# First batch of an attention and SwiGLU kernel: grouped softmax, moved weight rounding, Newton root

## Chip, cores and metric

The kernel runs on one core of a Trainium2 chip. The metric is the device time of one launch in microseconds (us); the profile's span is the profiled execution alone.

## The reference, cut to what matters

Attention with 32 learnt queries over 12,416 rows, then the rows attend to the 32 results, then a gated feed-forward layer on every row:

```python
B, N, m, C = 4, 12416, 32, 128          # x: (B, N, C); inducing: (m, C)
def mab(q, kv):
    s = scale * (q @ kv.transpose(0, 2, 1))
    s = s - s.max(-1, keepdims=True)
    a = np.exp(s)
    a /= a.sum(-1, keepdims=True) + 1e-09
    return a @ kv
h = mab(I, x)                            # I: inducing, once per batch
y = mab(x, h).reshape(B * N, C)
rms = np.sqrt(np.mean(y * y, axis=-1, keepdims=True) + 1e-06)
xn = y / rms * rms_g
g = xn @ w_gate                          # C -> 1536
out = (g / (1 + np.exp(-g))) * (xn @ w_val) @ w_out
```

`w_gate`, `w_val` and `w_out` come as 64-bit floats, the other inputs as 32-bit floats.

## The kernel before, in words

The 97 tiles of 128 rows of a batch form seven sets: five of 16 tiles (0 to 4), one of 15 (5) and one of 2 (6, the set that the code calls `full`). In the second attention and in the feed-forward layer a set is worked in units of up to 512 columns; a unit has 12 slots, one per 128 of the 1536 hidden channels. A slot does `g` (L677), silu on ACT (L685), `v` (L688), their product on DVE (L694), and adds products with `wo` (L613) to the unit's accumulator, either at once ("plain") or split in three faster products ("three", L629 to L670).

Every engine gets its instructions in the order in which the Python code issues them. For batches 1 to 3 all of the attention's steps are laid between the slots by `schedule` and the steps of a list of slot numbers; for batch 0 there is nothing yet to lay them between, so the main part (L703 to L803) writes out the order by hand. That part is the start, and it is what the change touches:

1. x comes in by SP's queue, set after set (`load_rows`), and set 6 in four pieces at the end. Between and behind them come the raw weights in chunks of 128x512 64-bit words (`fetch_raw`); five chunks have a place at once, the other four are fetched as places become free.
2. `turn_x` transposes a set's tiles on TensorE, four to a PSUM bank, and ACT copies each bank to SBUF (L316). There are five such banks. `scores1` multiplies with the 32 queries and DVE takes the scores out together with each row's maximum (L326).
3. `max1`, `max2`, `max3` bring the maximum over all sets to every partition: a reduction on DVE, a transpose on TensorE, two short operations on DVE, a product on TensorE, a copy. The bias of the exponential needs it, and so the exponentials (`exp1_of`, L355) begin after the last set's scores.
4. `turn_e` transposes the exponentials on DVE, `sum_h` adds their products with x in one bank (L378), `fold_l` adds the denominators, `divide` divides (L393), `turn_h` and `square_h` prepare the second attention.
5. The seam of set 0: scores, maximum, exponential, `turn_a`, `square`, `turn_z`, `scale`, `root` (on POOL, a power of -0.5, L516), `apply`, `turn_b`, `split`. Set 0's first unit gets its input `a` by `spread` (two products, one ACT copy, L558); the next two units get theirs by `gather`, four SBUF to SBUF transfers each on SP (L545).
6. Then the slots begin; slots 0 to 3 belong to unit 0, 4 to 7 to unit 1, 8 to 11 to unit 0 again, and so on for the first two units; set 0's later units begin at slot 24.

Rounding the weights to 32 bits (`rounding`) is a side job. A chunk's high word is cut by DVE into exponent (L249) and upper fraction (L262); ACT makes numbers of them (L229, L231; for two chunks DVE does so, L233); DVE puts the sign on (L271) and adds the low word (L277); POOL multiplies (L279) and `put` stores the chunk (L221, for `w_gate` and `w_val`) and fetches the next raw one. There are nine chunks, three of each weight, named (weight, chunk) in the order (0,0), (1,0), (2,0), (0,1), ... Five are rounded before the slots or in the first of them, four in slots 1 to 14. `stack_of` multiplies a rounded chunk with h to make the first layer's matrices for batch 0, `stack_low` takes a part of the rounding error off. `warm` issues idle matmuls.

A planner (`rehearse`) goes through all slots with a table of costs (`COST`) and decides which products take the three-product form and where in a slot products are issued. For batch 0 it allows the form from the third unit and slot 26 on.

## Time and profile before

| | |
|---|---|
| median of 3 runs | 1623.13 us (1622.79 to 1623.69) |
| span of the profiled execution | 1621.7 us |
| PE busy | 1604.3 us, 99% |
| DVE, ACT, POOL busy | 1444.6, 1238.3, 1217.7 us |
| first silu of the first slot | 56.02 us |
| last sum of h ends | 38.46 us |

PE is TensorE; PEld its weight loads, which overlap; DVE VectorE, ACT ScalarE, POOL GpSimd, SP the sync engine, whose queue issues most transfers. Busy time of a matmul is modelled from pipelined records, so a busy TensorE is one that has work queued. The mean of a line can mix shapes. The start takes 55 of 1622 us, and shares over the whole span hide it: it is read alone, by timelines and by stretches.

### The profile page before, as it was taken

How to read it: one execution, taken by the hardware profiler on the slowest of the kernel's cores; microseconds unless marked ns; L12 is line 12 of the kernel's file. 1: busy time of each engine (PE TensorE's matmuls, PEld its weight loads, DVE VectorE, ACT ScalarE, POOL GpSimd, SP SyncE). 2: the span in 40 equal slices, each digit the busy share in tenths (PEclk: the TensorE clock that was granted, in tenths of full speed). 3: DMA queues.
4: the chain of work that ended last, by engine and by line, in shares of the span. 5: the costliest groups of instructions: out<-in, count | busy, mean ns of one | idle time of the engine just before them, and what ended most of it. 6: DMA issues, size and time to landing. Idle time of an engine off the chain costs nothing.

```text
span 1621.7 us, 25435 instructions
## 1 busy us (share of the span) xinstructions
PE 1604.3 (99%) x7085; PEld 1085.6 (67%) x7085; DVE 1444.6 (89%) x2504; ACT 1238.3 (76%) x2285; POOL 1217.7 (75%) x979
## 2 busy tenths in 40 slices
PE   8999999999999999999999999999999999999998
PEld 6546666756676666766677666676667777777776
DVE  4879988999899998899899998789989999999997
ACT  4567877767887778776778777877778888878886
POOL 1358885878588886688678888587858878878876
PEclk9999999999999999999999999999999999999999
DMA  7455624444353141634445323353221122111221
GB/s 262 91 72 85 112 43 97 88 97 69 60 94 59 36 95 29 133 76 81 69 67 83 55 54 68 63 125 79 46 38 29 31 39 40 35 35 36 40 38 26
DMA packets 389181, 112.52 MB, mean 69 GB/s; under 512 B 365072, under 2 KB 369712, under 8 KB 386480
## 3 DMA queue, kind: packets, MB, share of 16 engines
q1 hardware_dynamic: 388304, 110.82, 34.8%
q8 instruction: 56, 0.92, 0.3%
q14 instruction: 85, 0.70, 0.2%
q10 hardware_dynamic: 736, 0.08, 0.0%
HBM read 53.95 MB, written 27.00 MB: 50 GB/s over the span
## 4 chain that ended last, share of the span: by engine, by line
PE 94%; DVE 1%; ACT 1%; issue 1%; POOL 0%; DVEq 0%; ACTq 0%
PE acc L613 35%; PE gv L677 18%; PE gv L688 16%; PE u L635 10%; PE u L633 10%; PE gv L322 3%; PE gv L499 1%; PE gv L378 1%; DVE gv L694 1%; ACT silu L685 1%; PE gv L453 0%; DVE xn L660 0%; PE gv L467 0%; DVE o L621 0%; POOL xn L279 0%
## 5 line engine op out<-in xcount | busy, mean ns | idle before, releaser
L669 POOL TENSOR_TENSOR xn<-xn,xn 128x512 fp32r<-128x512 f32 (+2 forms) x705 | 870.9, 1255 | 268.6 <-DVE xn L660 156.8
L685 ACT ACTIVATE silu<-gv 128x512 f32<-128x512 f32 (+2 forms) x1186 | 689.7, 586 | 258.4 <-PE gv L677 231.8
L688 PE MATMUL gv<-a,sv 128*128 128x512 f32 (+2 forms) x1188 | 636.1, 536 | 0.8 <-ACT silu L685 0.8
L613 PE MATMUL acc<-u,wo 128*128 128x512 f32 (+1 forms) x990 | 490.8, 581 | 0.0
L677 PE MATMUL gv<-a,sg 128*128 128x512 f32 (+2 forms) x1188 | 486.7, 410 | 1.5 <-ACT silu L685 0.8
L694 DVE TENSOR_TENSOR u<-silu,gv 128x512 f32<-128x512 f32 (+2 forms) x621 | 407.7, 663 | 51.7 <-PE gv L688 32.3
L694 DVE TENSOR_TENSOR gv<-silu,gv 128x512 f32<-128x512 f32 (+2 forms) x565 | 376.0, 668 | 66.1 <-PE gv L688 49.0
L660 DVE SCALAR_TENSOR_TENSOR xn<-xn,gv 128x512 fp32r<-128x512 f32 (+2 forms) x566 | 371.3, 656 | 9.5 <-ACT xn L659 5.9
L659 ACT ACTIVATE xn<-gv 128x512 fp32r<-128x512 f32 (+2 forms) x566 | 330.4, 584 | 43.1 <-DVE gv L694 30.9
L677 PEld LDWEIGHTS gv<-a,sg 128*128 128x128 f32 x1188 | 223.8, 188 | 189.4 <-ACT silu L685 40.2
L688 PEld LDWEIGHTS gv<-a,sv 128*128 128x128 f32 x1188 | 223.6, 188 | 139.6 <-issue 46.3
L613 PE MATMUL acc<-xn,more 128*128 128x512 f32 (+2 forms) x705 | 273.6, 388 | 3.0 <-DVE o L621 2.6
L633 PE MATMUL u<-xn,xn 128*128 128x512 f32 (+2 forms) x705 | 272.4, 386 | 0.0
L613 PEld LDWEIGHTS acc<-u,wo 128*128 128x128 f32 x990 | 184.9, 188 | 46.7 <-issue 9.1
L664 POOL TENSOR_TENSOR xn<-u,xn 128x512 fp32r<-128x512 f32 (+2 forms) x139 | 178.6, 1285 | 41.6 <-ACT xn L663 41.6
L635 PE MATMUL u<-xn,xn 128*128 128x512 f32 (+2 forms) x414 | 160.1, 387 | 0.0
L613 PEld LDWEIGHTS acc<-xn,more 128*128 128x128 f32 x705 | 132.4, 188 | 33.5 <-POOL xn L669 5.7
L633 PEld LDWEIGHTS u<-xn,xn 128*128 128x128 f32 x705 | 132.6, 188 | 28.6 <-issue 5.5
L663 ACT ACTIVATE xn<-u 128x512 fp32r<-128x512 f32 (+2 forms) x139 | 87.4, 629 | 36.6 <-DVE u L694 32.4
L635 PE MATMUL u<-xn,more 128*128 128x512 f32 (+2 forms) x291 | 112.5, 387 | 0.0
L516 POOL TENSOR_TENSOR rs<-ms,mhalf 128x16 f32<-128x16 f32 (+2 forms) x28 | 75.9, 2709 | 18.1 <-DVE ms L511 17.1
L635 PEld LDWEIGHTS u<-xn,xn 128*128 128x128 f32 x414 | 77.7, 188 | 17.5 <-DVE gv L694 0.2
(151 smaller groups left out, 1096.9 us busy)
## 6 DMA issues: line engine op xcount, KB each, us to landing
out_dram<-o SPq DMA_DIRECT2D x320, 64.0 KB, 2.0
xT<-in_x_dram SPq DMA_DIRECT2D x60, 256.0 KB, 5.4
xn<-in_x_dram SPq DMA_DIRECT2D x60, 256.0 KB, 5.0
a<-hi SPq DMA_DIRECT2D x156, 64.0 KB, 2.0
a<-lo SPq DMA_DIRECT2D x156, 64.0 KB, 2.0
xn<-in_x_dram SPq DMA_DIRECT2D x5, 1024.0 KB, 10.6
xn<-w SPq DMA_DIRECT2D x18, 256.0 KB, 3.6
out_dram<-o SPq DMA_DIRECT2D x64, 60.0 KB, 2.0
```

What stands on the lines that cost most here:

```text
L613: nc.tensor.matmul(acc[:, 0:T], lhsT, rhs, start=st["left"] == NJ, stop=st["left"] == 1)
L633: nc.tensor.matmul(ups[:, 0:T], weight_of(0, j), hi, start=st["k"] == nk, stop=False)
L635: nc.tensor.matmul(ups[:, 0:T], weight_of(1, j), lo, start=False, stop=not st["k"])
L659: nc.scalar.activation(hi, v, AF.Copy, scale=(1.0 - 2.0 ** -13) * 2.0 ** -12)
L660: nc.vector.scalar_tensor_tensor(out=lo, in0=hi.bitcast(F32), scalar=-4096.0, in1=v, op0=ALU.mult, op1=ALU.add)
L663: nc.scalar.activation(d, v, AF.Copy, scale=1.0 - 2.0 ** -13)
L664: nc.gpsimd.tensor_tensor(out=lo, in0=v, in1=d.bitcast(F32), op=ALU.subtract)
L669: nc.gpsimd.tensor_tensor(out=d, in0=hi.bitcast(F32), in1=lo.bitcast(F32), op=ALU.subtract)
L677: nc.tensor.matmul(g[:, 0:T], sg[:, ts(j, P)], a[:, 0:T], start=True, stop=True)
L685: nc.scalar.activation(sl[:, 0:T], g[:, 0:T], AF.Silu)
L688: nc.tensor.matmul(v[:, 0:T], sv[:, ts(j, P)], a[:, 0:T], start=True, stop=True)
L694: nc.vector.tensor_tensor(out=t[:, 0:T], in0=sl[:, 0:T], in1=v[:, 0:T], op=ALU.mult)
```

## The change

In words:

- Batch 0's first softmax is taken in three groups of sets (0 to 2, 3 and 4, 5 and 6), each with its own maximum, exponential and PSUM bank; `shares` computes exp(bias difference) for each group, and `divide` joins the three sums with these factors. The order of the start is written anew, with sums of early groups between the transposes of later sets.
- Set 6 is loaded first, from ACT's queue, and transposed after set 0. Set 5 is loaded in two parts. All raw weights are fetched after x.
- Every second bank of transposes is copied by DVE instead of ACT.
- Rounding a chunk is now two masks on DVE, four operations on ACT (power, upper part, sign, low word) and three on POOL (`join`); only (1,0) keeps the old joining with two DVE operations (`join_short`). Before the slots, (0,1) and (1,1) are rounded later than they were; within them the chunks are at slots 0 to 12 instead of 0 to 14.
- The root of the first seam is computed by an integer first guess and three Newton steps on DVE, 12 short operations.
- The planner's table follows; `wo` is split from slot 15 (17), and the three-product form is allowed from slot 25 (26).

The diff, cut:

```diff
+    GROUPS = (range(0, 3), range(3, 5), range(5, NS))
...
-                nc.sync.dma_start(out=t[ts(q, m), 0:n, :], in_=of(xrows, b, s)[q])
+                (nc.sync if b else nc.scalar).dma_start(out=t[ts(q, m), 0:n, :], in_=of(xrows, b, s)[q])
...
+        def join():
+            if wide:
+                e, f = st["e"].bitcast(F32), st["f"].bitcast(F32)
+                nc.gpsimd.tensor_tensor(out=f[:], in0=f[:], in1=st["low"].bitcast(F32), op=ALU.add)
+                nc.gpsimd.tensor_tensor(out=e[:], in0=e[:], in1=st["high"].bitcast(F32), op=ALU.mult)
+                nc.gpsimd.tensor_tensor(out=st["dst"], in0=f[:], in1=e[:], op=ALU.mult)
+            put()
...
-                nc.scalar.copy(out=dst, in_=src)
+                if k % 2:
+                    nc.vector.tensor_copy(out=dst, in_=src)
+                else:
+                    nc.scalar.copy(out=dst, in_=src)
...
+        def shares():
+            G = len(st["parts"])
+            least = small.tile([P, 1], F32, name="mx")
+            nc.vector.tensor_reduce(out=least[:], in_=st["nb"][:], axis=AX.X, op=ALU.min)
+            share = st["share"] = small.tile([P, G], F32, name="rl")
+            nc.scalar.activation(share[:], st["nb"][:], AF.Exp, bias=least[:], scale=-1.0)
+            ls = st["ls"][:, 0:G]
+            nc.vector.tensor_tensor(out=ls, in0=ls, in1=share[:], op=ALU.mult)
+            nc.vector.reduce_sum(out=st["hl"][:, C:C + 1], in_=ls, axis=AX.X)
...
+    def first_root(ms, rs):
+        n = small.tile([P, 16], I32, name="mx2")
+        y, t = rs, small.tile([P, 16], F32, name="mx2")
+        nc.vector.tensor_scalar(out=n[:], in0=ms.bitcast(I32), scalar1=1, scalar2=None, op0=ALU.logical_shift_right)
+        nc.vector.tensor_scalar(out=y.bitcast(I32), in0=n[:], scalar1=-1.0, scalar2=float(0x5F3759DF),
+                                op0=ALU.mult, op1=ALU.add)
+        nc.vector.tensor_scalar_mul(out=ms, in0=ms, scalar1=-0.5)
+        for _ in range(3):
+            nc.vector.tensor_tensor(out=t[:], in0=y, in1=y, op=ALU.mult)
+            nc.vector.tensor_tensor(out=t[:], in0=t[:], in1=ms, op=ALU.mult)
+            nc.vector.scalar_tensor_tensor(out=y, in0=t[:], scalar=1.5, in1=y, op0=ALU.add, op1=ALU.mult)
...
+    turn_x(0, *range(R))
+    f["scores1"](0)
+    turn_x(NS - 1, 0)
+    turn_x(1, *range(R))
+    f["scores1"](NS - 1)
+    turn_x(2, *range(R))
+    f["scores1"](1)
+    f["scores1"](2)
+    f["max1"](0)
+    turn_x(3, *range(R))
+    f["max2"]()
+    f["max3"](0)
+    f["exp1_of"](0, 3, 0)
+    f["scores1"](3)
+    f["turn_e"](0)
+    turn_x(4, *range(R))
+    f["sum_h"](0)
+    f["scores1"](4)
+    f["max1"](1)
+    turn_x(5, 0, 1)
+    f["max2"]()
+    turn_x(5, 2, 3)
+    f["max3"](1)
+    f["exp1_of"](3, 5, 1)
+    f["turn_e"](1)
+    f["scores1"](5)
+    f["max1"](2)
+    f["sum_h"](1)
+    f["turn_e"](2)
+    f["max2"]()
+    weight[0, 0]["masks"]()
+    f["sum_h"](2)
+    f["max3"](2)
+    numbers(0, 0)
+    f["exp1_of"](5, NS, 2)
+    f["turn_e"](3)
+    f["sum_h"](3)
+    f["turn_e"](4)
+    f["sum_h"](4)
+    weight[0, 0]["join"]()
+    f["turn_e"](5)
+    f["turn_e"](6)
+    f["shares"]()
+    weight[1, 0]["masks"]()
+    f["fold_l"]()
+    f["sum_h"](5)
+    f["sum_h"](6)
+    numbers(1, 0, False)
+    for g in range(len(GROUPS)):
+        f["divide"](g)
     f["turn_h"]()
     ps = f["scores"](0, f["st"]["hT"][:, 0:m], R, per2[0])
     f["square_h"]()
-    weight[2, 0]["sign"]()
-    f["stack_of"](0, 0)
+    weight[1, 0]["join_short"]()
     warm(10)
     f["scores2"](0, ps)
+    f["stack_of"](0, 0)
     f["row_max"](0)
     f["sub_max"](0)
-    weight[2, 0]["lower"]()
+    weight[2, 0]["masks"]()
     f["exp2"](0, 1)
     tiny = small.tile([P, 1], F32, name="tiny")
     nc.scalar.activation(tiny[:], ones, AF.Silu)
+    numbers(2, 0)
+    weight[2, 0]["join"]()
     turn_a, square, turn_z, scale, root, apply, turn_b, split = seam(0, 0)
     turn_a()
     square()
-    parts(0, 1)
+    weight[0, 1]["masks"]()
     f["stack_of"](1, 0)
-    warm(26)
+    warm(20)
     turn_z()
     scale()
     root()
-    weight[0, 1]["sign"]()
-    for i in range(2):
-        f["stack_low"](i, 0)
-    parts(1, 1)
     apply()
     turn_b()
     split()
     spread(0, 0)
+    numbers(0, 1)
+    weight[0, 1]["join"]()
+    for i in range(2):
+        f["stack_low"](i, 0)
     warm(3)
     gather(0, 1)
     gather(0, 2)
-    weight[0, 1]["lower"]()
+    weight[1, 1]["masks"]()
+    numbers(1, 1)
+    weight[1, 1]["join"]()
...
-            for k, one in ((1, (2, 1)), (5, (0, 2)), (8, (1, 2)), (11, (2, 2))):
-                for j, name in ((0, "power"), (1, "power_number"), (1, "upper"), (2, "upper_number"), (2, "sign"), (3, "lower")):
-                    add(k + j, weight[one][name])
-            for k, *one in ((2, 0, 1), (4, 1, 1), (11, 0, 2), (13, 1, 2)):
+            for k, one in ((0, (2, 1)), (3, (0, 2)), (6, (1, 2)), (9, (2, 2))):
+                for j, name in enumerate(("masks", "power_number", "upper_number", "sign_number", "lower_number", "join")):
+                    add(k + (j + 1) // 2, weight[one][name])
+            for k, *one in ((2, 0, 1), (4, 1, 1), (9, 0, 2), (12, 1, 2)):
```

## The prediction

> **What bounds the kernel now.** I read the page first: its chain of waits says what ends last.
>
> ```profile
> span 1621.7 us, 25435 instructions
> ...
> PE 94%; DVE 1%; ACT 1%; issue 1%; POOL 0%; DVEq 0%; ACTq 0%
> ```
>
> TensorE is the bound, and nothing in the change takes matmuls out of the long middle. So the question is when TensorE gets into its stride. Busy time by stretches shows the stages of the start (columns: stretch, its length, PE, PEld, DVE, ACT and POOL busy with counts, clock, DMA share, GB/s):
>
> ```profile
> 8.17:25.64 17.47, 16.02 (x140) 11.35 (x138) 5.25 (x15) 12.08 (x25) 0.00 (x0) 1.00 1.00 395
> 25.64:31.53 5.89, 5.41 (x50) 4.32 (x50) 5.50 (x17) 1.91 (x4) 1.27 (x1) 1.00 0.40 109
> 31.53:38.46 6.93, 6.70 (x197) 5.43 (x196) 5.44 (x13) 3.37 (x8) 1.29 (x1) 1.00 0.29 83
> 38.46:54.25 15.79, 13.30 (x92) 10.19 (x91) 13.54 (x25) 6.52 (x13) 4.56 (x2) 1.00 0.19 64
> 54.25:62.40 8.15, 7.65 (x26) 4.40 (x27) 6.29 (x11) 4.86 (x9) 2.76 (x3) 1.00 0.55 148
> ...
> 110.00:1600.00 1490.00, 1485.71 (x6315) 1008.67 (x6314) 1354.57 (x2325) 1167.82 (x2152) 1178.95 (x934) 1.00 0.34 64
> ```
>
> Transposes and scores; the maximum's chain (most of that TensorE time is warm-up matmuls); the sums of h; the seam, a chain through DVE; the first slots. Past 110 us TensorE idles 4.3 us in 1490. A microsecond won or lost before about 62 us therefore stays won or lost at the end.
>
> Then the timelines of DVE, POOL, ACT and SP, one by one, around the change's places (start, length, engine, line, operation):
>
> ```profile
> 48.12 0.68 DVE L271 SCALAR_TENSOR_TENSOR we<-sg,we 128x512 int32<-128x512 int32 x1
> ...
> 59.99 0.92 DVE L262 TENSOR_SCALAR o<-sc 128x512 int32<-128x512 int32 x1
> ```
>
> ```profile
> 48.29 3.29 POOL L516 TENSOR_TENSOR rs<-ms,mhalf 128x16 f32<-128x16 f32 x1 [3.25 <-DVE ms L511]
> ...
> 54.98 1.28 POOL L279 TENSOR_TENSOR xn<-o,we 128x512 f32<-128x512 f32 x1 [3.40 <-PE gv L555]
> ...
> 59.28 1.34 POOL L279 TENSOR_TENSOR xn<-o,we 128x512 f32<-128x512 f32 x1 [2.88 <-PE gv L677]
> ```
>
> ```profile
> 54.84 0.58 ACT L558 CAST a<-gv 128x512 fp32r<-128x512 f32 x1 [2.98 <-PE gv L555]
> ...
> 56.02 1.58 ACT L685 ACTIVATE silu<-gv 128x512 f32<-128x512 f32 x3 [0.59 <-PE gv L677]
> ```
>
> ```profile
> 58.00 0.59 SPq L545 DMA_DIRECT2D xn<-lo  x1
> 58.69 0.53 SPq L221 DMA_DIRECT2D w<-xn  x1
> 59.31 0.40 SPq L209 DMA_DIRECT2D sg<-in_moe_w_out_dram  x1
> ```
>
> Three things to see. ACT has nothing between the copy of `a` and the first silu. The store of the weight that POOL finished at 56.26 goes out at 58.69, behind the eight gathers written ahead of it: SP keeps the program's order. And L262, whose median is 0.42, takes 0.92 while a POOL operation runs to 60.62, and ends 0.29 after it.
>
> **What the skill says.** SBUF — State Buffer, "Who interferes with whom": DVE and GpSimd share a port pair, a lock for a whole instruction; one-source DVE operations in a 2-port mode and those with two SBUF inputs contend. The trace agrees for the first kind (0.92 above; L249 has 0.90 and 0.80 beside POOL); for the second it hints: the power after L271 took 3.29, the median of its line is 2.90. PSUM — Partial Sum Buffer, "Engine vs sequencer instructions": ScalarE, VectorE and GpSimd queues are strict FIFO; every timeline here follows program order. DMA: Bandwidth & Descriptors, "Queues, rings and completion order": each DMA engine takes turns between queues. The trace agrees: `gam`, 0.5 KB on ACT's queue behind `ind`, needed 8.8 us, and between 4.5 and 10.0 us its queue moved 144 packets beside x.
>
> **The change, part by part.** Before and after are walked down the program's order with durations of this trace, an instruction starting when its engine is free and its inputs are there. For the kernel before this gives the division at 39.3; it ended at 38.87. I subtract the 0.4 below.
>
> *Three groups, copies on two engines.* TensorE's work up to the last sum: 97 transposes at 0.115 (11.2), scores 97/16 x 0.97 (5.9), sums 97 x 0.065 (6.3), small products about 0.9: 24.3. From 8.17 that ends at 32.5 without waits. The order has these waits, 6.0 together: 0.9 for the copies of set 0; 1.2 before the first `max3` (DVE still has set 2's scores and two copies of set 3, 0.6 to 0.75 each, ahead of the two row operations); 0.5 before set 5's scores; 0.5 before set 2's sum; 1.2 before set 3's sum, since `exp1_of` of group two waits for group two's bias while DVE is busy; 0.9 before `fold_l`, since group three's exponential stands behind four rounding operations of 0.5 to 0.63 on ACT, and `shares` is four short dependent steps; the rest small. A DVE copy of 128x512 from PSUM is not in the trace: taken as 0.66 from L326, the same form with a maximum; 0.55 to 0.75 moves the sum by under 1 us. With the last two divisions (0.75) the division ends at 39.3 - 0.4 = 38.9. So the hidden chain (4.8 us, 26.7 to 31.5) is paid back in DVE's longer queue: 0, between -4 (half of the waits overlap more than I think, the exponential is not delayed) and +1.
>
> *Set 6 on ACT's queue, asked for right after set 0.* Before it landed at 22.7 and nobody waited. Now its 128 rows follow `gam` (10.0) in ACT's queue, in turn with x's packets of 8 KB (0.31 each): eight rounds per engine, 2.5 to 5 us, so about 13.5. TensorE reaches `turn_x` of set 6 at 11.85: +1.7. If a piece has to wait on ACT for an older transfer to land (SP did so at 6.07 and 10.0), ACT's table load and copies slip too: the walk then gives +2.0. Bounds 0 and +5. Fetching the weights behind x gains nothing here: x's sets 1 to 5 are transposed at TensorE's pace already.
>
> *Port lock in `shares`.* POOL's three products of weight (0,0), 1.25 each, run just then. The product `ls x share` and the two masks behind it meet two of them: +1.5 (0 to 1.7).
>
> *Seam.* Joining (1,0) puts two 0.6 operations on DVE ahead of the transpose of the scores, masks (2,0) two of 0.42 ahead of `turn_a`; part lies under the scores and the exponential: +0.4. Root: before, from the end of `scale` to `apply`, 48.21 to 51.62, 3.4. Now 12 dependent DVE operations on 128x16: L511 is 0.17 and L168's chain of small additions 0.25 a step, so 0.2 each, 2.4 alone. But ACT's table load and four roundings of (2,0) end at 47.9, and POOL's three products run 47.9 to 51.8, all over the root, each holding the port: about three steps get through, nine follow, 1.8: root takes 5.2. +1.8. Together +2.2; -0.6 without the lock.
>
> *First slots.* Let L be the end of `split` (54.24 before). The copy of `a` starts at L+0.6. Behind it ACT now has the four roundings of (0,1) (0.63, 0.52, 0.5, 0.5; Sign and the strided copy are not in the trace, taken as L231's, 0.5 to 0.65) and of (1,1): the first silu starts at L+5.4 instead of L+1.8. TensorE fills its banks with three g and two v, then waits. `stack_of` (0,1) at slot 2 needs POOL's three products, L+3.4 to L+7.15. And the store of (0,1) and the next fetch stand on SP ahead of both gathers: 0.53 + 0.40 from L+7.2, four gathers at 0.6, 2.0 to landing: `a` of unit 1 is there at L+12.0. Slot 4, the first of unit 1, starts at L+12.1; before it started at 59.51, L+5.3. Lost: 6.8, less two waits of before for weights (0.37 and 0.23) that go: +6.2. Bounds: 3.9 if the gathers were not held (stack_of alone), 7.5 with slower POOL products on strided words. If TensorE's clock drops in these gaps (TensorE: Matmul & The Clock Gate, Part 1, says after about 3.4 us idle; no run shows it, the clock here is 1.00 throughout), up to 3 more as an estimate.
>
> *Middle.* DVE has 1.35 less and ACT 1.1 more per chunk, POOL 2.5 more where it has little to do; TensorE bounds these slots. One more slot may take the three-product form, which saves 0.16: -0.2 (-1 to +1, since the planner's choices shift).
>
> Sum: 0 + 1.7 + 1.5 + 2.2 + 6.2 - 0.2 = +11.4 against the profiled execution's 1621.7; the other runs stand 1.4 above it (median 1623.13), so **1634.5**.
>
> **Rivals.** (a) The lock does not bite short operations: -1.5 and -2.8, so +7.1, 1630.2; the four long cases speak against it, that no operation of 16 elements is among them for it. 25%. (b) Set 6 in time and gathers barely held: 0 + 1.5 + 2.2 + 3.9 - 0.2 = +7.4 at most, with (a) +3.1. 10%. (c) Faster: the groups hide the chain wholly, -4, and the Newton steps are free of the lock, -0.6, and the roundings do not stand ahead of the first slots because ACT and SP don't keep the written order, so that the +6.2 goes: -4.8, 1618.3. It decides once the first slots lose under 1.4; the stores at 58.69 speak against it. 6%. (d) The change does not reach what it says: hidden chain and lost slots cancel, within 3 us. 5%. The forecast: 54%.
>
> A difference under 0.2% (3.2 us) cannot be told from none. Range: (b) with (a) at the bottom, 1626.2; the clock and a late set 6 at the top, +18: 1641. Faster 0.06, same 0.05, slower 0.89.
>
> **What would show it.** In the profile after: silu's first start over 4 us after the copy of `a`; on SP the L221-like store ahead of the gathers, and `a` waiting for it; TensorE idle in two gaps there; single short Newton operations of about 1 us beside POOL's; TensorE idle before set 6's transposes. Wrong if the first g of unit 1 starts under L+8, or if `split` ends before 54.

## The result, and the profile after

The changed kernel takes 1646.45 us (median of four runs, 1642.93 to 1647.26) against 1623.08 for the kernel before in the same measurement: a ratio of 1.0139, 95% interval 1.0122 to 1.0157. It is slower, as forecast, but by 23.4 us and not by 11.4, and outside the range. The profiled execution, the slowest of the four, has a span of 1645.3. First the page, its span and the shares of the chain of waits:

```profile
span 1645.3 us, 25416 instructions
...
PE 94%; DVE 3%; ACT 1%; DMA 1%; issue 1%; POOL 0%; ACTq 0%; SPq 0%; DVEq 0%; POOLq 0%
```

TensorE is still the bound, but DVE and DMA have risen in the chain: 3% and 1% of 1645 us. Then the busy times by stretches (stretch, length, PE, PEld, DVE, ACT, POOL busy with counts, clock, DMA share, GB/s): up to before's end of the transposes, up to the last division, the seam, the first slots up to slot 4, the middle:

```profile
8.17:25.64 17.47, 13.31 (x107) 9.35 (x105) 8.49 (x20) 5.25 (x10) 0.00 (x0) 0.90 1.01 392
25.64:45.04 19.40, 14.07 (x257) 10.01 (x249) 14.44 (x37) 9.61 (x17) 3.80 (x3) 0.97 0.07 21
45.04:66.32 21.28, 14.47 (x79) 10.28 (x79) 15.51 (x33) 6.09 (x13) 5.09 (x4) 0.82 0.25 83
66.32:81.06 14.74, 8.88 (x21) 4.92 (x20) 8.76 (x13) 9.96 (x18) 10.68 (x10) 0.72 0.29 82
110.00:1600.00 1490.00, 1484.98 (x6298) 1000.77 (x6296) 1350.08 (x2313) 1161.47 (x2130) 1163.84 (x922) 1.00 0.35 65
```

The middle is as it was (TensorE busy 1485.0 of 1490, before 1485.7). Everything is lost before 92 us. The clock column is new: 0.90, 0.97, 0.82, 0.72, where before had 1.00 everywhere.

Three marks in TensorE's timeline measure the stages: the turn of h (the product of `turn_h`, the end of stage 1), the first product of `spread` (the end of the seam), and the g-product of slot 10.

| | turn of h | spread | slot 10 | stage 1 | seam | spread to slot 10 |
|---|---|---|---|---|---|---|
| before | 38.92 | 53.66 | 68.91 | | 14.74 | 15.25 |
| after | 45.10 | 65.74 | 92.25 | +6.2 | 20.64 (+5.9) | 26.51 (+11.3) |

The lag at slot 10 is 23.3; at the last g-product of the kernel it is 23.6. Now the same timelines as before, at the same places (start, length, engine, line, operation, in brackets the idle time before it and what ended that). TensorE:

```profile
13.40 3.73 PE L315 MATMUL gv<-ident,xn 128*128 128x128 f32 x18 [1.85 <-DMA xn<-in_x_dram]
...
48.59 3.51 PE L185 MATMUL acc<-ident 128*128 128x128 f32 x20
51.94 1.02 PE L493 MATMUL gv<-lo,hg 128*128 128x512 f32 x2
...
65.74 0.77 PE L597 MATMUL gv<-hi,u 128*128 128x512 f32 x1 [4.32 <-DVE hi L574]
```

The wait for set 6 is there, 1.85. The 18 transposes behind it take 3.73, 0.207 each where before each took 0.115; the 20 warming products at 48.59 take 3.51 (2.39 before). DVE:

```profile
40.85 0.67 DVE L374 TENSOR_TENSOR gmx<-gmx,rl 128x3 f32<-128x3 f32 x1 [0.36 <-ACT rl L372]
...
41.63 1.50 DVE L243 TENSOR_SCALAR u<-sc 128x512 int32<-128x512 int32 x1
...
58.33 0.97 DVE L550 TENSOR_SCALAR ms<-ms 128x16 f32<-128x16 f32 x1
59.33 1.22 DVE L511 TENSOR_SCALAR mx<-ms 128x16 int32<-128x16 int32 x1
60.58 0.17 DVE L512 TENSOR_SCALAR rs<-mx 128x16 int32<-128x16 int32 x1
60.67 1.25 DVE L514 TENSOR_SCALAR ms<-ms 128x16 f32<-128x16 f32 x1
```

and POOL beside the root:

```profile
57.97 1.29 POOL L267 TENSOR_TENSOR u<-u,sc 128x512 f32<-128x512 f32 x1 [8.89 <-ACT sc L262]
59.22 1.30 POOL L268 TENSOR_TENSOR u<-u,sc 128x512 f32<-128x512 f32 x1
60.60 1.28 POOL L269 TENSOR_TENSOR wo<-u 128x512 f32<-128x512 f32 x1
```

A step on 16 elements per partition takes 0.17 alone; when it meets a POOL product, it lasts until that product ends: L550 ends with L267, L511 with L268, L514 with L269; L512 slips in at 60.58, just before L269 starts. ACT, in the seam and behind the copy of `a`:

```profile
52.99 0.59 ACT L494 CAST sg<-gv 128x512 fp32r<-128x512 f32 x1 [3.33 <-PE gv L493]
53.48 0.63 ACT L465 ACTIVATE sc<-sc 128x512 f32<-128x512 f32 x1
...
67.21 0.59 ACT L600 CAST a<-gv 128x512 fp32r<-128x512 f32 x1 [8.86 <-PE gv L597]
67.69 0.72 ACT L249 ACTIVATE u<-u,columns 128x512 int32<-128x512 int32 x1
...
72.18 1.06 ACT L727 ACTIVATE silu<-gv 128x512 f32<-128x512 f32 x2
```

The first silu starts 5.0 us after the copy of `a`, as forecast. The first line was not in the forecast: the seam's exponential (L465) stands on ACT behind the copy of stack (0, 0), which waits for TensorE, although DVE had its input ready at 50.44. SP:

```profile
74.06 0.33 SPq L223 DMA_DIRECT2D w<-xn  x1
74.48 1.40 SPq L211 DMA_DIRECT2D sg<-in_moe_w_out_dram  x1
75.97 0.62 SPq L587 DMA_DIRECT2D a<-hi  x1
```

Store and fetch stand ahead of the gathers, and slot 4's g-product starts at 81.06, after 2.86 us of waiting for `a`.

### The profile page after: what moved, and what is told of

It reads as the page before. It is cut to its first block, busy times and chain, and to the rows that moved or that the text cites. A ratio compares the mean times of both kernels' runs of the same rounds, so it can differ in the third digit from the quotient of the medians.

```text
span 1645.3 us, 25416 instructions
## 1 busy us (share of the span) xinstructions
PE 1610.5 (98%) x7049; PEld 1086.3 (66%) x7049; DVE 1455.2 (88%) x2520; ACT 1245.2 (76%) x2291; POOL 1234.3 (75%) x993
## 4 chain that ended last, share of the span: by engine, by line
PE 94%; DVE 3%; ACT 1%; DMA 1%; issue 1%; POOL 0%; ACTq 0%; SPq 0%; DVEq 0%; POOLq 0%
PE acc L655 34%; PE gv L719 17%; PE gv L730 16%; PE u L677 9%; PE u L675 9%; PE gv L327 3%; PE gv L538 1%; PE gv L396 1%; PE gv L315 1%; DMA xn<-in_x_dram 1%; DVE gv L736 1%; ACT silu L727 1%; PE gv L479 0%; DVE xn L702 0%; DVE u L736 0%
## 5 line engine op out<-in xcount | busy, mean ns | idle before, releaser
L706 POOL TENSOR_TENSOR xn<-u,xn 128x512 fp32r<-128x512 f32 (+1 forms) x138 | 177.3, 1284 | 41.7 <-ACT xn L705 41.7
L705 ACT ACTIVATE xn<-u 128x512 fp32r<-128x512 f32 (+1 forms) x138 | 86.8, 629 | 35.9 <-DVE u L736 31.6
L710 ACT ACTIVATE xn<-xn 128x512 fp32r<-128x512 f32 (+1 forms) x138 | 85.9, 623 | 0.0
```

What stands on the lines that cost most here:

```text
L705: nc.scalar.activation(d, v, AF.Copy, scale=1.0 - 2.0 ** -13)
L706: nc.gpsimd.tensor_tensor(out=lo, in0=v, in1=d.bitcast(F32), op=ALU.subtract)
```

## Experiments

All runs were timed beside the kernel before, in four executions each (all taken out: 5, best parts: 10, copies alone: 21); the ratio is to that. The three marks are from the profile of one of these executions.

| run | median us | ratio, 95% interval | turn of h | spread | slot 10 | seam | to slot 10 |
|---|---|---|---|---|---|---|---|
| changed | 1646.45 | 1.0139 [1.0122, 1.0157] | 45.10 | 65.74 | 92.25 | 20.64 | 26.51 |
| gathers first | 1642.97 | 1.0121 [1.0106, 1.0136] | 42.65 | 63.39 | 87.87 | 20.74 | 24.48 |
| last roundings | 1644.75 | 1.0131 [1.0116, 1.0146] | 44.76 | 65.45 | 88.44 | 20.69 | 22.99 |
| the same, slot 1 | 1641.86 | 1.0117 [1.0101, 1.0132] | 43.85 | 64.48 | 87.00 | 20.63 | 22.52 |
| stack ahead | 1643.41 | 1.0122 [1.0107, 1.0137] | 44.62 | 63.08 | 87.52 | 18.46 | 24.44 |
| root without POOL | 1641.93 | 1.0115 [1.0098, 1.0132] | 42.32 | 59.94 | 86.06 | 17.62 | 26.12 |
| full clock | 1641.15 | 1.0115 [1.0098, 1.0132] | 42.56 | 60.79 | 85.20 | 18.23 | 24.41 |
| set 6 later | 1640.98 | 1.0112 [1.0097, 1.0127] | 41.72 | 62.32 | 86.75 | 20.60 | 24.43 |
| shares without POOL | 1642.05 | 1.0119 [1.0103, 1.0134] | 42.98 | 64.19 | 88.68 | 21.21 | 24.49 |
| old slots | 1639.31 | 1.0098 [1.0084, 1.0112] | 45.11 | 65.78 | 84.42 | 20.67 | 18.64 |
| exponential first | 1640.75 | 1.0108 [1.0092, 1.0123] | 41.17 | 60.62 | 85.09 | 19.45 | 24.47 |
| all taken out | 1633.74 | 1.0065 [1.0053, 1.0078] | 40.85 | 56.52 | 79.58 | 15.67 | 23.06 |
| copies alone | 1624.54 | 1.0013 [1.0007, 1.0020] | 40.81 | 55.56 | | 14.75 | |
| short joins | 1642.52 | 1.0116 [1.0102, 1.0130] | 40.59 | 60.23 | 83.98 | 19.64 | 23.75 |
| old slots, full clock | 1639.92 | 1.0103 [1.0089, 1.0117] | 46.33 | 67.55 | 86.88 | 21.22 | 19.33 |
| best parts | 1626.54 | 1.0023 [1.0014, 1.0033] | 38.79 | 55.48 | 71.44 | 16.69 | 15.96 |

Two things about reading it. The turn of h moves by up to 4.0 us between kernels whose stage 1 is the same code (42.32 to 46.33), because set 6 lands at another time in every execution, with or without a stretch of half clock behind it; so a part's worth is read from its own stage, not from the median. The run with the gathers first shows the danger: its edit gains nothing by slot 10, and its median is still 3.5 under the changed kernel's. And the first slots, the same code in four of the runs, take 24.43 to 24.49 there (at full clock 24.41); the changed profile's 26.51 has some 2 us more. Of these, 1.2 have come by slot 4, where `a` lands later, and 0.9 come after it: there TensorE is at half clock up to 84.9 us, and from slot 4's g-product to slot 5's it takes 3.23 in place of 1.85.

### Gathers first on SP

```diff
     spread(0, 0)
+    gather(0, 1)
+    gather(0, 2)
     numbers(0, 1)
     weight[0, 1]["join"]()
...
-    gather(0, 1)
-    gather(0, 2)
```

> The changed kernel with one thing moved: the gathers of units 1 and 2 stand on SP ahead of the store and the fetch that end the rounding of chunk (0, 1). Theory A (SP's order holds the gathers: the store waits for POOL's last product, 74.06 us, and the gathers start at 75.97): they start within 1 us of the split, slot 4's g-product loses its wait of 2.86 us on the gather, and the kernel takes 2.9 us less than the changed one, 1643.5. Theory B (the roundings on ACT and POOL set slot 4 whatever SP does): slot 4 waits elsewhere for the same time, change under 0.7 us. Theory C (the gathers are slow by themselves, behind the weights' fetches): they start early but land after 78 us, gain under 1 us.

TensorE, slot 4's g-product and the stack of slot 9:

```profile
76.02 0.39 PE L719 MATMUL gv<-a,sg 128*128 128x512 f32 x1
...
87.31 1.13 PE L493 MATMUL gv<-xn,hg 128*128 128x512 f32 x2 [1.13 <-POOL xn L269]
```

Slot 4 no longer waits for `a`: it starts 12.6 us after `spread`, in the runs with untouched slots 14.1. But slot 10 is at 24.48, where those have 24.43 to 24.49: at slot 9's stack TensorE waits for POOL's join and the gain is gone. Of the 4.4 us between this profiled execution (1642.86) and the changed one (1647.26), 2.45 are stage 1's (turn of h at 42.65) and 2.0 the excess of the changed profile's first slots. SP's order does hold slot 4, as Theory A says, but only for 1.5 us, and by slot 10 nothing is left of them, as Theory B says.

### The last two roundings as before

```diff
     weight[0, 1]["masks"]()
+    numbers(0, 1, False)
     f["stack_of"](1, 0)
...
-    numbers(0, 1)
-    weight[0, 1]["join"]()
...
     gather(0, 2)
-    weight[1, 1]["masks"]()
-    numbers(1, 1)
-    weight[1, 1]["join"]()
+    weight[0, 1]["join_short"]()
```

with masks and conversions of (1, 1) in slots 0 and 1 and its short join in slot 2; in the second run they are in slot 0 and the join in slot 1.

> The changed kernel with the last two roundings as in the kernel before: chunk (0, 1)'s two conversions before the root and its short join after the gathers, chunk (1, 1) in slots 0 to 2 with the short join. Theory A (first slots lose because eight conversions on ACT stand ahead of the first silu and two long POOL joins ahead of the second stack): first silu under 1.5 us after the copy of a (4.97 now), slot 4's g-product 6 us after the end of the split instead of 14.74, total 1646.4 - 9 = 1637.5. Theory B (the TensorE clock, at half in 64.4 to 71.2 and 74.7 to 78.1, makes most of it): silu early, but slot 4 still 10 us after the split, total about 1642.

> The changed kernel with the last two roundings as before, as in the run with both moved, but chunk (1, 1)'s short join in slot 1, not slot 2. There slot 4's g-product was 7.6 us earlier than in the changed kernel and then waited 3.4 us at the next stack for POOL's product of chunk (1, 1), whose two VectorE steps stood behind slot 2's product. Theory A (only that wait took the gain back): the stack of (1, 1) waits under 0.5 us, slot 5 keeps 7 us or more, total 1646.4 - 7 = 1639. Theory B (the gain is given back in slots 5 to 12 by the later roundings, long joins beside VectorE's masks): slot 4 is 7 us earlier but slot 14 only 3.5, total 1643.

With the join in slot 2, slot 4's g-product came 8.0 us after `spread` (15.3 in the changed profile), and the next stack waited 3.40 for POOL. The first silu came 1.7 after the copy of `a`, near Theory A's 1.5, but the median is far from its 1637.5. With the join in slot 1:

```profile
75.78 1.10 PE L493 MATMUL gv<-xn,hg 128*128 128x512 f32 x2 [0.60 <-ACT silu L727]
...
86.44 1.13 PE L493 MATMUL gv<-xn,hg 128*128 128x512 f32 x2 [1.09 <-POOL xn L269]
```

```profile
76.50 1.47 DVE L243 TENSOR_SCALAR we<-sc 128x512 int32<-128x512 int32 x1
77.90 1.51 DVE L245 TENSOR_SCALAR o<-sc 128x512 int32<-128x512 int32 x1
```

That stack's wait for POOL is gone and slot 4 stands at 9.1. Yet slot 10 is at 22.5, only 2.0 under 24.5. The second fence shows a part of the reason: the masks of the next chunk take 1.5 each on DVE beside the long join, not 0.41, and the later stack waits 1.09 for that chunk's join. Theory B of the second run: given back in slots 5 to 10.

### The stack of (0, 0) ahead of the warming products

```diff
+    f["stack_of"](0, 0)
     warm(10)
     f["scores2"](0, ps)
-    f["stack_of"](0, 0)
```

> The changed kernel with the stack of chunk (0, 0) issued before the ten warming products again, as in the kernel before. Theory A (its copy on ACT stood ahead of the exponentials and waited for TensorE to finish the warming products at half clock): the exponentials start within 0.4 us of the subtraction of the maxima (3.0 now), the end of the split comes 2.6 to 3.0 us earlier, total 1643.6. Theory B (the seam's other side, the clock and the square's wait on TensorE, ends at the same time anyway): exponentials earlier, split earlier by under 1 us, total 1646.

```profile
50.20 0.59 ACT L494 CAST sg<-gv 128x512 fp32r<-128x512 f32 x1 [1.02 <-PE gv L493]
50.69 0.63 ACT L465 ACTIVATE sc<-sc 128x512 f32<-128x512 f32 x1
```

The exponential starts 0.7 us after the maxima are subtracted (at 49.96), not 3.0, and the seam is 2.2 shorter. Theory A holds, under its 2.6 to 3.0: of the 2.3 won by the exponential, the `square` product, which stood on TensorE behind the warming products, took 0.9 back, and the root returned 0.8, because in this profile two of its steps met a POOL product and not three (1.28 and 1.12 us).

### Nothing on POOL beside the root

```diff
     numbers(2, 0)
-    weight[2, 0]["join"]()
...
     split()
+    nc.gpsimd.tensor_copy(out=tiny[0:1, :], in_=split_of[0, 0][1].bitcast(F32)[0:1, 0:1])
+    weight[2, 0]["join"]()
     spread(0, 0)
```

> The changed kernel with the POOL join of chunk (2, 0) held until the split's lo half is written (a POOL copy of one element reads it), so that nothing runs on POOL beside the Newton root. Theory A (the slow Newton steps of 0.97, 1.22 and 1.25 us are slow because POOL holds the shared port): each takes under 0.25 us, from the start of the scaling to the row product 2.5 us instead of 5.4, split 2.9 us earlier, total 1643.6. Theory B (those three steps are slow for a reason of their own, as integer and scaled forms): they keep their time, total 1646 to 1647. Theory C (gained in the root, lost again because the moved join delays chunk (0, 1)'s join and so the second stack): split 2.9 earlier, slot 4 less than 1 us earlier.

```profile
55.38 0.18 DVE L550 TENSOR_SCALAR ms<-ms 128x16 f32<-128x16 f32 x1
55.59 0.17 DVE L511 TENSOR_SCALAR mx<-ms 128x16 int32<-128x16 int32 x1
...
57.90 0.69 DVE L562 TENSOR_TENSOR sc<-sc,rs 128x512 f32<-128x512 f32 x1
```

From scaling to row product 2.52 us, not 5.37; seam 3.0 shorter. Theory A: the slow steps are slow because of POOL and for no reason of their own. That is the lock that the Trainium skill describes (SBUF — State Buffer, "Who interferes with whom"), on operations of 16 elements too. A part of Theory C is there as well: the first slots take 26.12, 1.7 over the runs that leave this join alone. The moved join holds slot 2's stack (a wait of 1.74 for POOL), slot 4 starts 0.8 later after `spread`, and behind it the clock is at half.

### Full clock

Nothing moved; warming products in TensorE's gaps (`warm(8)` ahead of set 6 and of `fold_l`, `warm(7)` ahead of `turn_h`, `warm(20)` to `warm(38)`, and two groups in slots 2 and 4).

> The changed kernel with nothing moved, but warming products of 0.11 to 0.24 us put in TensorE's idle stretches: 8 ahead of set 6's transposes, 8 ahead of the row-sum fold, 7 ahead of the turn of h, 18 more in the root, 9 ahead of slot 2's second product, 12 ahead of slot 4's first. Theory A (the half clock, 24 us in the changed profile, costs time of its own: set 6's transposes 1.6, the seam's warming products, scores and turn 1 to 2, the first slots 1 to 2): no half clock in 10 to 90 us, total 4 to 5.5 us under the changed kernel, 1641.5. Theory B (the waits decide, the clock only stretches work that is hidden in them): clock full, total within 1 us, 1645.5 to 1647.

```profile
25.64:42.50 16.86, 15.03 (x263) 11.63 (x256) 12.74 (x34) 7.17 (x14) 3.83 (x3) 1.00 0.08 23
42.50:61.50 19.00, 16.12 (x118) 12.80 (x116) 15.52 (x34) 6.08 (x13) 5.10 (x4) 1.00 0.29 95
61.50:75.70 14.20, 10.43 (x62) 7.96 (x62) 8.53 (x12) 9.97 (x18) 10.60 (x9) 1.00 0.32 89
```

The clock is 1.00 in each stretch, the seam 2.4 shorter, the first slots 24.41, as in the four runs whose half clock ends ahead of slot 4. Theory A for stage 1 and the seam; Theory B for the first slots, where TensorE waits anyway.

When the clock drops can be read from the profiles together. Within a profile every change of the clock lies on a grid of 3.41 us: in the changed one the drops are at 13.22, 43.94, 64.42, 74.66 and 81.48, which are 9, 6, 3 and 2 times 3.41 apart. Cut the time from 7 to about 95 us of the 15 profiles that have half clock into such steps, and take the share of each step in which TensorE was busy (as modelled). All 26 steps with at most 0.41 were followed by a step at half clock, none of the 257 with at least 0.53 was, and of the 19 between, 13 were. The steps with set 6's wait in the changed run, in "exponential first" and in "the same, slot 1", two lines each (columns as above):

```profile
9.81:13.22 3.41, 1.07 (x8) 0.19 (x8) 1.23 (x3) 0.00 (x0) 0.00 (x0) 1.00 1.03 393
13.22:16.63 3.41, 3.23 (x16) 3.26 (x16) 0.69 (x1) 0.96 (x2) 0.00 (x0) 0.50 0.98 407
...
8.72:12.13 3.41, 1.53 (x13) 0.41 (x11) 1.71 (x4) 0.59 (x1) 0.00 (x0) 1.00 1.03 399
12.13:15.54 3.41, 3.31 (x16) 3.34 (x17) 0.69 (x1) 1.00 (x3) 0.00 (x0) 0.50 1.01 418
...
8.51:11.92 3.41, 1.64 (x14) 0.52 (x12) 1.82 (x4) 0.58 (x1) 0.00 (x0) 1.00 1.01 397
11.92:15.33 3.41, 1.67 (x15) 1.70 (x16) 0.34 (x1) 0.96 (x2) 0.00 (x0) 1.00 1.01 415
```

A wait of 1.11 us (the second run) was enough, since it shared its step with 0.87 of waiting for a copy: TensorE was busy for 1.53 of 3.41, a share of 0.45. A wait of 2.65 (the third) fell across two steps, left 0.48 and 0.49 in them, and did nothing. So where a gap lies on the grid counts beside its length.

### Set 6 after set 2

```diff
-    turn_x(NS - 1, 0)
     turn_x(1, *range(R))
-    f["scores1"](NS - 1)
...
     f["max1"](0)
+    turn_x(NS - 1, 0)
+    f["scores1"](NS - 1)
     turn_x(3, *range(R))
```

> The changed kernel with set 6's transposes and scores after set 2's instead of after set 0's; its data lands at 13.2 us, when TensorE still works on sets 1 and 2. Theory A (the wait for set 6 costs 0.3 to 2.6 us and, where it is over 0.9, the clock window after it another 1.6): no wait over 0.3 us ahead of any set, clock full to 40 us, the turn of h starts at 41.9 to 42.3 in this and in every profile, 45.1 in the changed one; total 1643.5 and a smaller spread. Theory B (set 1's or 2's own landing takes the place of that wait): the turn of h not before 43.5, total 1646.

No wait for x is left, and the turn of h is at 41.72: 3.4 under the changed profile, 1.85 of it the wait and 1.5 the half clock behind it (in three runs at full clock set 6's transposes start 30.2 us before the turn of h, in the changed profile 31.7). Theory A. The four executions lie within 1.4 us; those of the runs that keep the wait lie within 1.7 to 4.3. The wait itself varies: it was 0.33, 0.43, 1.05, 1.11, 1.50, 1.71, 1.76, 1.85, 2.47, 2.58 and 2.65 in the profiles with the changed order.

### Nothing on POOL beside the shares, and the last exponential first

```diff
-    weight[0, 0]["join"]()
...
         f["divide"](g)
+    tiny = small.tile([P, 1], F32, name="tiny")
+    nc.gpsimd.tensor_copy(out=tiny[:], in_=f["st"]["hn"][:, 0:1])
+    weight[0, 0]["join"]()
     f["turn_h"]()
```

and in the second run, with that:

```diff
-    numbers(0, 0)
     f["exp1_of"](5, NS, 2)
...
     f["shares"]()
+    numbers(0, 0)
```

> The changed kernel with POOL's join of chunk (0, 0) held until the last division (a POOL copy of one column reads its result), so that POOL is idle beside the shares. Theory A (the shared port: the product of sums and shares took 0.67, chunk (1, 0)'s first mask 1.50 beside POOL): 0.2 and 0.41, the reciprocal starts 1.8 us after the exponential of the shares ends instead of 2.6, the turn of h 1.1 to 1.5 us earlier after the last score's exponential, total 1645. Theory B (the fold and the last set's sums on TensorE set the end of the stage): VectorE shorter, the turn of h under 0.4 us earlier, total unchanged.

> The changed kernel with chunk (0, 0)'s four conversions on ACT behind the last exponential of stage 1 instead of ahead of it, and its POOL join held until the last division. Theory A (the three groups lose by this order: ACT's conversions, 2.4 us, hold the last exponential, and the port lock holds the shares): from the last copy of a maximum (37.20 in the changed profile) to the turn of h 5.4 us instead of 7.9, of which 0.5 is given back in the seam where the later join slows VectorE's steps for chunk (1, 0); total 1644.5. Theory B (only the lock matters, as the run with the held join showed, 1.5 us): 6.4 us, total 1645.3. Theory C (TensorE's sums of sets 3 to 6 set the end): 7 us or more.

DVE in the first of the two:

```profile
40.33 0.16 DVE L374 TENSOR_TENSOR gmx<-gmx,rl 128x3 f32<-128x3 f32 x1 [0.36 <-ACT rl L372]
...
40.60 0.42 DVE L243 TENSOR_SCALAR u<-sc 128x512 int32<-128x512 int32 x1
```

0.16 for 0.67 and 0.42 for 1.50. From the copy of the last maximum (37.20 in the changed profile, 36.67 here, 36.07 in the second run) to the turn of h it is 7.90, 6.31 and 5.10 us: the lock was 1.6, and ACT's order another 1.2. Theory A in both. The seam gives some of it back, since the moved join meets the next steps on DVE, here in the second run:

```profile
42.62 1.79 DVE L275 SCALAR_TENSOR_TENSOR u<-sc,u 128x512 int32<-128x512 int32 x1
44.34 1.75 DVE L277 SCALAR_TENSOR_TENSOR u<-sc,u 128x512 f32<-128x512 uint32 x1
```

which take 0.68 each alone. These have two SBUF inputs, the second kind that the skill's section names as contending; the forecast had only a hint of it. In the first run the seam grows by 0.6. In the second it shrinks by 1.2 all the same: with stage 1's shorter gaps TensorE is busy for 0.72 of the clock's step ahead of the turn of h (0.51 in the first run), and the turn and the scores run at full clock (1.06 us for the eight products of the scores, 1.94 in the first).

### The first slots as before, and the same at full clock

From `split` on the order of the kernel before: `sign`, `lower` and `join_short` at their old slots, stacks and weight splits too. In the second run also `warm(20)` to `warm(38)`.

> The changed kernel with everything from the split on as in the kernel before: the roundings of the second, third and fourth chunks with the short join at the old slots, the stacks and the weight splits at the old slots, the gathers ahead of chunk (0, 1)'s last step; stage 1 and the seam stay as changed. Theory A (the first slots lose by the long joins: POOL holds the shared port for 3.9 us a chunk and VectorE's masks beside it take 1.5 us instead of 0.41, besides ACT's conversions ahead of the silus): from the end of the split to slot 10's g-product 15 us (before 14.7, changed 25.9), total 1646.4 - 10.5 = 1636. Theory B (the half clock, or the later start of the weights' data, keeps the slots slow): 18 us or more, total over 1638.5.

> The run with the first slots as in the kernel before, and 18 more warming products in the root, so that TensorE has no idle stretch of 4 us ahead of the split. Theory A (the 3.3 us that the first slots still lost there were the half clock of 64 to 71 us): from the end of the split to slot 10's g-product 15 to 15.8 us (18.6 without the warming products), total 3 us less than that run's 1639.3, 1636.5. Theory B (they are ACT's two conversions for chunk (1, 1) and VectorE's masks ahead of the first silus): over 17.5 us, total within 1 us.

18.64 from `spread` to slot 10: 5.8 less than 24.45, but 3.4 more than before. From the end of the split it is 18.1: Theory A's 15 is missed, and the number is Theory B's. The second run has full clock from about 53 to 74 us, its first three slots included (a g-product takes 0.40 there, 0.63 in the changed profile), and takes 19.33: not the clock of these slots, and Theory B again. Its timelines show what it is, DVE, ACT and TensorE:

```profile
70.69 0.42 DVE L241 TENSOR_SCALAR u<-sv 128x512 int32<-128x512 int32 x1
71.03 1.63 DVE L247 TENSOR_SCALAR u<-sv 128x512 int32<-128x512 int32 x1
```

```profile
72.69 0.63 ACT L260 ACTIVATE u<-u 128x512 f32<-128x512 int32 x1 [0.83 <-DVE u L247]
73.23 1.55 ACT L741 ACTIVATE silu<-gv 128x512 f32<-128x512 f32 x3
```

```profile
73.86 0.79 PE L744 MATMUL gv<-a,sv 128*128 128x512 f32 x1 [2.55 <-ACT silu L741]
```

Before, the masks of (1, 1), both `stack_low` and a `sign` ran on DVE while POOL computed the root. The Newton root takes DVE itself, so these 2.8 us of work stand behind the split; the last mask meets a POOL product, ACT's conversion waits for the mask, and the silus wait behind the conversion. That this is most of the 3.4 is borne out by the last run below, which has POOL's root again and the old slots: 15.96.

### Short joins throughout

Every `join` becomes `join_short`, every `numbers(i, c)` becomes `numbers(i, c, False)`, places unchanged.

> The changed kernel with every long POOL join (three products, four conversions on ACT) replaced by the short one (two conversions, two VectorE steps of 0.68, one POOL product), all at the same places in the order. Theory A (the common cause is POOL's hold of the shared port for 3.9 us a chunk, and ACT's extra conversions): root steps 0.17, masks 0.41 except beside the one product, first silu 1.2 us earlier, total 6 to 8 us under the changed kernel, 1639.5, although VectorE has 1.36 us more work for each of nine chunks. Theory B (the order of the steps, not the joins, costs the time; VectorE's added steps take the place of what the joins cost): within 2 us of 1646.4.

The median is 3.9 under the changed kernel, between the theories, but no more than gathers first has, which gains nothing by slot 10. Root steps 0.17, as Theory A says. But DVE, with the joins' two steps on it at ACT's pace, now waits for ACT: 3.65 us in the seam and 1.83 behind the split, and slots 5 to 10 still have 1.5 us masks beside the one POOL product that is left. So the long joins are not the whole of it; where the steps stand costs time too.

### All losses taken out

The edits above in one kernel: set 6 later, the last exponential first, the stack ahead, warming products, old slots, and the join of (2, 0) after (0, 1)'s last step.

> All losses taken out together: set 6 after set 2, conversions of (0, 0) behind the last exponential and its join behind the last division, 8 and 7 warming products in stage 1's gaps and 26 in the root, the stack of (0, 0) ahead of the ten warming products, no POOL work beside the Newton root, first slots as before. The three groups, the Newton root, the copies on two engines and the data queues stay as changed. Theory A (the losses are the five mechanisms and nothing else): turn of h at 39.4 (before 38.9), split at 54.5 (before 54.2), slot 10 at 69.5 (before 68.9), clock full throughout; total within 2 us of the kernel before, 1624. Theory B (something of the change that none of these takes out costs more): slot 10 at 73 or later, total 1627 or more.

It fell short: 1633.7, 10.8 over the kernel before, by its numbers Theory B. Root and clock are as expected (0.17 a step; 1.00 in the seam). But I mis-sized two edits. The eight and seven warming products run to 37.76 and 40.85, while what they bridge is ready at 35.96 and 39.7: together up to 3 us. So the run does not decide between the theories. And the join, now late, holds the first projection:

```profile
66.72 2.07 PE L669 MATMUL acc<-u,wo 128*128 128x512 f32 x2 [3.43 <-POOL wo L275]
```

### The copies alone, on the kernel before

```diff
-                nc.scalar.copy(out=dst, in_=src)
+                if k % 2:
+                    nc.vector.tensor_copy(out=dst, in_=src)
+                else:
+                    nc.scalar.copy(out=dst, in_=src)
```

> The kernel before with one part of the change alone: every second copy of the transposed x is done by VectorE. Theory A (two waits of TensorE on ACT's copies, 0.83 and 0.62 us, are shortened): the last score 0.4 to 0.6 us earlier, total 0.4 less than the kernel before. Theory B (the transposes on TensorE set stage 1): same to 0.2 us. Theory C (the copies hold VectorE's masks and scores): 0.3 to 1 us more.

```profile
26.57 2.04 PE L325 MATMUL gv<-xT,indT 128*32 128x480 f32 x16 [2.02 <-DVE xT L317]
```

1.9 us later at the turn of h and 1.6 in the median, more than Theory C's 1: the last copies stand on DVE behind five steps of chunk (0, 0), which were off the path before. The 21 executions form two groups, 11 at 1624.0 to 1624.5 and 10 at 1625.8 to 1626.4, so that the 1.6 stands for neither. The profile is of the second group and has a step at half clock from 26.62 to 30.03, in which these 16 products take 2.04 (1.12 before); whether that step is what parts the groups is not shown.

### Best parts

Three groups with set 6 later and the exponential first, short joins, POOL's root with DVE's steps in its shadow, old slots.

> What of the change showed a gain, with the rest as in the kernel before: three groups with set 6 after set 2, chunk (0, 0)'s conversions behind the last exponential, data queues and copies as changed; short joins, POOL's root with VectorE's displaced steps in its shadow, the old first slots. Theory A (the three groups are worth about 1 us once nothing stands in their way): turn of h at 37.8 to 38.3 (before 38.9), 0.5 of it given back to (0, 0)'s and (1, 0)'s steps in the seam, slot 10 at 68.4 to 69.5 (before 68.9), total 1622 to 1623.5. Theory B (the roundings displaced from stage 1 into the seam cost more than the groups bring): slot 10 at 70.5 or later, total 1624.5 or more.

Theory B. The turn of h is at 38.79, where before has 38.92: the groups gain nothing even with what stood in their way removed, against my 1 us. The copies on two engines, which cost 1.9 alone, are still in it; groups without them were not run, so a gain that the copies hide is not ruled out. The displaced steps of (0, 0) and (1, 0) lengthen the seam by 1.95, 1.06 of it here:

```profile
52.38 1.75 DVE L573 TENSOR_TENSOR sc<-sc,rs 128x512 f32<-128x512 f32 x1
```

a product of 0.69 beside POOL's product for (2, 0). With 1626.5 it is 20 us under the changed kernel, so the parts that it takes back hold most of the loss, and 3.7 over the one before. No version that I ran beats the kernel before.

## Why the forecast was right and wrong

**Direction, and four terms of the sum, right.** Middle: -0.2 forecast, +0.3 measured. Set 6's wait: 1.7 forecast, 1.85 here; as the wait was 0.33 to 2.65 from profile to profile, to hit it so closely was luck, though the middle one of the eleven waits is 1.71. Lock in `shares`: 1.5 forecast, 1.6. Root: 3.4 to 5.2 forecast, so +1.8; 3.58 to 5.37 measured from the start of the scaling, 1.8 too. Rival (a), a lock that doesn't bite short operations, is refuted by the run with the root alone; (c) by SP, ACT and POOL keeping the written order.

**Size, wrong by half, in four places:**

1. *Seam, "+0.4" for all but the root; measured 4.1.* I costed what the change adds to DVE and passed over a step that it moves: `stack_of` of (0, 0), behind the warming products. Its copy stands on ACT ahead of the exponential and waits for TensorE: 2.9 (exponential 3.0 after its input, before under 0.1), of which undoing the move gives 2.2 back. The other 1.2 come before the exponential's input is ready, with the turn of h and the scores at half clock.
2. *The clock, kept out of the sum as "up to 3 more" in the first slots.* It cost nothing there in four runs and about 0.9 in the changed profile, behind slot 4; it cost 1.5 in stage 1 and 2.4 in the seam (where it overlaps with the stack's 2.9, since the warming products at half clock are what the copy waits for). The forecast looked for long gaps. The Trainium skill (TensorE: Matmul & The Clock Gate, Part 1) speaks of an idle window of about 3.4 us; the length agrees with the grid of 3.41 here, but the window need not be idle: a busy share of up to 0.41 was always enough, and seven of the nine waits of 1.05 to 2.65 us for set 6 were followed by half clock.
3. *Stage 1's order on ACT.* The groups and copies were forecast at 0, with the exponential behind four conversions as one of several waits, 0.9, that the hidden chain pays for. It was 1.2 on top. With set 6's 1.85, the clock's 1.5 and the lock's 1.6 that makes up the 6.2 of the stage.
4. *First slots, +6.2 up to slot 4 and nothing after.* The mechanisms are all there: silu 5.9 us after the split (5.4 forecast), SP's order, POOL's join. But slot 4 came 14.7 after the split, not 12.1, and slots 4 to 10 took 11.2 against 9.4: "DVE has 1.35 less ... TensorE bounds these slots" failed, for masks beside a long join take up to 1.5 and not 0.41, which eats what DVE saves. Of the 9.2 that the first slots lose in most profiles, the old order returns 5.8; the other 3.4 are for the most part the steps that the Newton root displaces, which I gave a place but no cost. The gathers' order, which I took for the last holder, is worth 1.5 at slot 4 and 0 at slot 10.

By stage: 3.2 forecast and 6.2 measured, 2.2 and 5.9, 6.2 and 11.3.

What stays open: which of the steps with a share of 0.42 to 0.52 bring half clock; and why the fetch's issue on SP took 1.40 in the changed profile and 0.39 in the four runs with the same slots. The gathers behind it start 10.2 us after `spread` there and 9.2 in those runs, which is 1.0 of the 1.2 us by which slot 4 is later.

## What to carry to other kernels

When a step is moved, walk it on each engine that it issues to: a copy that lands ahead of a short operation on an in-order queue costs what the copy waits for. Work taken off one engine and given to another that holds it up is not taken off: price each of the first engine's operations beside it at the longer time (here masks at 1.5 and not 0.41). An idle gap is priced with what follows it: seven of the nine waits of over 1 us for set 6 were followed by 3.4 us or more of half clock. And an operation that waits on another engine may be the room in which other work is done for nothing; making it faster on the busy engine takes the room away.

## What the hardware showed that I had not expected

- A VectorE operation of 16 elements per partition (0.17 us) lasts until the POOL product that it meets has ended, 0.96 to 1.28 us; the three in the changed kernel's root end within 0.05 us of it.
- VectorE operations with two SBUF inputs go from 0.68 or 0.69 to 1.75 and 1.79 beside POOL, masks with one from 0.41 to 1.5.
- The half clock comes in stretches of one or more steps of 3.41 us, on one grid per profile, 24 us in all in the changed one; a step with TensorE busy for at most 0.41 of it always brought it, one with 0.53 or more never did.
- The wait for a small transfer asked for at the same place in the code was 0.33 to 2.65 us from profile to profile.
